# When the second layer of an expert runs, and when the weights' product is spread between the experts

## The chip, the cores and the metric

The kernel runs on one core of one Trainium2 chip. The metric is the device time of one execution in microseconds (us). Three runs of the kernel before gave 395.93, 396.1 and 394.4, a median of 395.93. Five engines work side by side: TensorE (PE, with its weight loads as PEld), VectorE (DVE), ScalarE (ACT), GpSimd (POOL), and SyncE (SP), which here only issues transfers. Sixteen DMA engines move the data.

## The reference, cut to what matters

Three blocks follow each other on 4608 tokens (8 batches of 576) with 512 features, all in fp32:

```python
# 1. retention: 8 batches, 8 heads, 576 positions, 64 features a head
ret = (q @ k.T / 8) * Dmat          # Dmat[i, j] = gamma_h ** (i - j), 0 above the diagonal
x = ret @ v                         # as 4608 x 512
# 2. soft mixture: 8 experts with 4 slots each
logits = x @ phi                                    # 4608 x 32
d = softmax(logits, over tokens); c = softmax(logits, over slots)
slot_in = d.T @ x                                   # 32 x 512
h = relu(slot_in[e] @ w1[e]); slot_out[e] = h @ w2[e]   # w1[e] 512 x 1024, w2[e] 1024 x 512
x = c @ slot_out                                    # 4608 x 512
# 3. bilinear block
out = (((x @ m1) * (x @ m2)) @ w3) @ w_out          # m1, m2 512 x 1024, w3 1024 x 1024, w_out 1024 x 512
```

The inputs of m1, m2, w3 and w_out come as 64-bit floats, the expert weights as fp32.

## The kernel before, in words

The kernel has four stages. Stage 1 (`for u in range(NU)`) does the retention, 36 units of 128 tokens, with the softmax over tokens beside it. Stage 2 is the loop over the eight experts (`for e in range(NE)`, L938 to L965), about 171 to 250 us in the profile; the change is in it alone. Stage 3 (about 250 to 285 us) makes use of the rank: after the experts, x is c times a 32-row matrix, so the bilinear block needs only products of pairs of slot rows. They are formed on VectorE (`pairs`, L1040 to L1047) and multiplied with the product of the last two weights, `w3 @ w_out` (`g_mm`, L1055). Stage 4 (285 to 395 us) does nine blocks of 512 tokens with the result (L1121 to L1136).

In stage 2 three kinds of work share TensorE, in the order in which the loop writes them; every engine and SP's list of transfers work in program order, nothing is sorted afterwards.

* **The experts.** `emit_l1(e)` (L602) multiplies the 4 slots with the first layer's weights, 16 matmuls, which the trace shows as 32; ScalarE applies relu (L607), VectorE transposes (L615, called at step t = 1). `emit_l2(e)` (L622) is the second layer, 8 matmuls shown as 16. An expert's weights are eight transfers of 512 KB (L583, `load_expert`), four for each layer. They go into a ring of buffers that were q, k, v and other tiles in stage 1 (hence names as `q<-in_ew`, `xts<-in_ew`). A buffer goes back to the list `free` when the layer that reads it is written down, so the transfer into it waits for that layer's matmuls; the first buffer of each second layer leaves the ring for good (`wplaces`).
* **The weights' product.** `emit_Ws(n)` writes n of 64 groups of `w3 @ w_out`, three matmuls of 128 x 512 each (L564): weights are held as a high and a low half, and three of the four cross products are taken. Eight groups fill a PSUM bank, which ScalarE and VectorE then evict (L572, L573). Three groups stand ahead of the experts.
* **The conversion.** A piece of w3 (64-bit, 512 KB, L479) is turned into fp32 and its two halves by two operations on ScalarE (L502, L504), three on VectorE (L503, L505, L497), an addition on GpSimd (L523), a copy on ScalarE (L528) and a subtraction on GpSimd (L533). `convert(n)` writes n of the five first ones; `tick()` writes the addition, the copy and the subtraction at a later step. The transfer of the next piece is written directly behind the last VectorE operation of an earlier one (L497), since it overwrites the raw data.

Each expert has four steps t = 0 to 3. At each step the loop runs `tick`, issues what transfers it can, calls `emit_Ws` up to a target number of groups, then the second layer at its step, then one step of the token softmax (`soft`: PE transposes L409 and L390, VectorE L396 and L397, ScalarE L398 and L410), then `convert`. SP's list is in that order too: a transfer whose wait isn't over keeps all later ones back. Its transfers use eight semaphores in turn, so that a transfer also waits for the eighth before it to have landed.

Of the kernel before, what the change touches and what calls it, by code (L numbers as in the profile page):

```python
# [31 lines left out]
def retention_softmoe_bilinear(  # L32
# [65 lines left out]
    def place(tag, name=None, dt=F32):  # L98
        t = new("place", name or tag, 1024, dt, tag=tag)
        all_places.append((t, tag))  # L100
        return t

    def tag_of(t):
        return next(g for x, g in all_places if x is t)
# [310 lines left out]
    def store_expt(last):  # L415
        for T, n in ((0, 8), (8, 1)):
            for g in range(4):
                for o in (0, 32):
                    i = nc.sync.dma_start(
                        out=bass.AP(expt.tensor, expt.offset + 512 * (64 * T + o) + 128 * g, [[512, 32], [64 * 512, n], [1, 128]]),  # L420
                        in_=L["et"][T // 8][32 * g:32 * g + 32, 0:n],
                    )
                    if T + g + o == 0:
                        after(i, last)
# [56 lines left out]
    def load_pieces():  # L481
        while nl[0] < len(pieces) and nl[0] < done[0] + NRAW:
            load_piece(nl[0])
            nl[0] += 1
# [4 lines left out]
    def conv_list(i):  # L489
        t, p = value(turn[i]), parts[i % 2]  # L490
        w = raws[i % NRAW].rearrange("p (n w) -> p n w", w=2)
        lo, hi = w.bitcast(U32)[:, :, 0], w.bitcast(U32)[:, :, 1]
        tu = t.bitcast(U32)
        v = nc.vector

        def last():
            v.scalar_tensor_tensor(out=tu, in0=hi, scalar=0xC0000000, in1=tu, op0=ALU.bitwise_and, op1=ALU.bitwise_or)  # L497
            done[0] += 1
            adds.append(lambda: add(i))

        return [
            lambda: nc.scalar.activation(out=t, in_=w[:, :, 1], func=ACTF.Abs),  # L502
            lambda: v.tensor_scalar(out=t, in0=t, scalar1=W_MIN, scalar2=W_MAX, op0=ALU.max, op1=ALU.min),  # L503
            lambda: nc.scalar.activation(out=p.bitcast(I32), in_=lo, func=ACTF.Copy, scale=2.0 ** -29),  # L504
            lambda: v.tensor_scalar(out=tu, in0=tu, scalar1=3, scalar2=0x3FFFFFFF, op0=ALU.logical_shift_left, op1=ALU.bitwise_and),  # L505
            last,
        ]

    def run_conv(n):
        for _ in range(min(n, len(conv_ops))):  # L510
            conv_ops.pop(0)()
# [32 lines left out]
    nsplit, nW = [0], [0]  # L544
# [7 lines left out]
    def emit_Ws(n, lag=1):  # L552
        for _ in range(n):
            i, k = divmod(nW[0], 4)
            if i == 16 or nsplit[0] < min(9 + i + lag, 24):
                return
            nW[0] += 1
            ps = bank[(5, 2)[i // 2 % 2]]
            b = block(w3p, i % 3)
            ah, al = (b[:, o + 128 * k:o + 128 * k + 128] for o in (0, 512))  # L560
            k8 = 4 * (i % 2) + k
            bh, bl = (t[:, 512 * k8:512 * k8 + 512] for t in (woh, wol))
            for part, (x, y) in enumerate(((ah, bh), (ah, bl), (al, bh))):
                nc.tensor.matmul(out=ps, lhsT=x, rhs=y, start=(k8 == 0 and part == 0), stop=(k8 == 7 and part == 2))  # L564
            if k8 == 7:
                evicts.append(lambda cb=i // 2, ps=ps: evict(cb, ps))

    def evict(cb, ps):
        t = place(tag_of(wplaces[cb]), f"w{cb}", F32R)
        wh.append(t[:, 0:512])  # L570
        wl.append(t[:, 512:1024])
        nc.scalar.copy(out=wh[cb], in_=ps)  # L572
        nc.vector.tensor_tensor(out=wl[cb], in0=ps, in1=wh[cb], op=ALU.subtract)  # L573
# [4 lines left out]
    def load_expert(n=1):  # L578
        loads = []
        while n and free and len(ew) < 8 * NE:  # L580
            e, j = divmod(len(ew), 8)
            ew.append(free.pop(0))
            loads.append(nc.sync.dma_start(out=ew[-1], in_=(ew1, ew2)[j // 4][e][:, 1024 * (j % 4):1024 * (j % 4) + 1024]))  # L583
            n -= 1
        return loads
# [12 lines left out]
    def emit_l1(e):  # L598
        ps = bank[e % 2]
        for k in range(4):  # L600
            for g in range(4):
                last = nc.tensor.matmul(  # L602
                    out=ps[32 * g:32 * g + 32, 0:256], lhsT=slotm[:, 128 * e + 32 * k:128 * e + 32 * k + 32],
                    rhs=ew[8 * e + k][:, 256 * g:256 * g + 256], start=(k == 0), stop=(k == 3), skip_group_check=True,
                )
        hr = tmp.tile([128, 256], F32, tag="h0", name="hr")
        nc.scalar.activation(out=hr, in_=ps[:, 0:256], func=ACTF.Relu)  # L607
        hr_of[e] = hr
        free.extend(ew[8 * e:8 * e + 4])
        return last  # L610

    def emit_turned(e):
        hr = hr_of[e]
        ht = tmp.tile([128, 256], F32, tag="h1", name="ht")
        nc.vector.transpose(out=ht, in_=hr)  # L615
        ht_of[e] = ht

    def emit_l2(e):
        ht = ht_of[e]
        for cb in range(8):  # L620
            qd = cb % 4
            nc.tensor.matmul(  # L622
                out=bank[4][32 * qd:32 * qd + 32], lhsT=ht[:, 32 * cb:32 * cb + 32], rhs=ew[8 * e + 4 + cb // 2][:, 512 * (cb % 2):512 * (cb % 2) + 512],
                start=(e == 0 and cb < 4), stop=(e == 7 and cb >= 4), skip_group_check=True,
            )
        free.extend(ew[8 * e + 4:8 * e + 8])
# [28 lines left out]
    with tc.manual_schedule():  # L655
# [75 lines left out]
        def can_conv():  # L731
            if nconv[0] == nl[0]:
                return False
            j = turn[nconv[0]]
            return 8 <= j < N3 or nth(j) < nsplit[0] + 3
# [167 lines left out]
        def convert(n):  # L903
            while n:
                if not conv_ops:
                    if not can_conv():
                        return
                    conv_ops.extend(conv_list(nconv[0]))
                    nconv[0] += 1
                    run_conv(1)  # L910
                run_conv(1)
                n -= 1
                if adds:
                    load_pieces()

        def tick():
            run(subs)
            run_copies()
            run(adds)
            run(evicts)  # L920
# [4 lines left out]
        def soft():  # L925
            T, step = divmod(nsoft[0], 2)
            if T < NT:
                nsoft[0] += 1
                if step == 0:
                    emit_csoft(T)  # L930
                else:
                    emit_expt(T)
                    if T + 1 < NT:
                        emit_turn(T + 1)
# [3 lines left out]
        for e in range(NE):  # L938
            load_expert(8)
            last = emit_l1(e)  # L940
            if e == NE - 1:
                store_expt(last)
            if e == 0:

                free[:] = [t for t in free if not any(t is x for x in ring)]
                second = tag_of(free.pop(0))
                etp = [place("ew0", "et0"), place(second, "et1")]
                L["et"] = [t.rearrange("p (t n) -> p t n", n=128) for t in etp]
                L["soft"] = [etp[1][:, o:o + 128].rearrange("p (g s) -> p g s", g=4) for o in (512, 640)]
            for t in range(4):  # L950
                tick()
                if t == 1:
                    emit_turned(e)
                load_expert(8)
                emit_Ws(max(0, min(55, 4 + (4 * e + t + 1) * 52 // 28) - nW[0]))
                if e == NE - 1 and t == 1:
                    emit_Ws(3, 0)
                if t == 2:
                    emit_l2(e)
                    if len(wplaces) < 8:  # L960
                        wplaces.append(free.pop(0))
                    load_expert(8)
                while e < NE - 1 and nsoft[0] <= (4 * e + t) * 18 // 28:
                    soft()
                convert(2 + t % 2)  # L965
        emit_Ws(1, 0)
        so = acc
        nc.scalar.copy(out=so[:, 0:256], in_=bank[4][:, 0:256])
# [245 lines left out]
```

## Time and profile before

| what | value |
|---|---|
| runs (us) | 395.93, 396.1, 394.4, median 395.93 |
| the profiled execution, its own time | 397.17 us, span 395.4 us |
| PE busy | 377.4 us (95%), 4447 matmuls |
| PEld busy | 284.3 us (72%) |
| DVE, ACT, POOL busy | 254.5, 198.8, 172.5 us (64, 50, 44%) |
| chain that ended last | PE 72%, DMA 13%, DVE 11% |
| main DMA queue | 107.85 MB, 85.3% of 16 engines |
| granted clock of TensorE | 0.999 |

The page gives busy shares over the whole span; the four stages have different limits. The chain that ended last is followed back from the last instruction, so it names what released each step. The profiled execution lies 1.24 us above the median of the runs.

### The profile page before, as it was taken

The page shows a single profiled execution, that of the slowest core. Times are in us where ns is not written, and L with a number is a line of the kernel's source. Part 1 is how long each engine was busy: PE and PEld are TensorE (multiplying, and loading weights), DVE is VectorE, ACT ScalarE, POOL GpSimd, SP SyncE. Part 2 cuts the span into 40 slices and gives each one's busy share as a digit, 9 for nine tenths or more (in the row PEclk, how much of TensorE's full clock was granted, in tenths as well). Part 3 has the DMA queues.
Part 4 walks back from the last instruction along what each step waited for, and adds up shares of the span by engine and source line. Part 5 has one row for each costly group of instructions (what it writes and reads, how often), then busy time and mean ns, then how long its engine had stood idle before and what let it go on. Part 6 is the DMA issues. An engine that isn't in the chain of part 4 may idle for free.

```text
span 395.4 us, 10962 instructions
## 1 busy us (share of the span) xinstructions
PE 377.4 (95%) x4447; PEld 284.3 (72%) x4447; DVE 254.5 (64%) x432; ACT 198.8 (50%) x424; POOL 172.5 (44%) x158
## 2 busy tenths in 40 slices
PE   6999998999998999899999998999999999999995
PEld 3889786878887886566555553578687777788774
DVE  3458999899887988545776552299766443555410
ACT  2347695788676785414544521235444353444332
POOL 2732765675554554113554431037634434553420
PEclk9999999999999999999999999999999999999999
DMA  7999999799889999997999999692269979999543
GB/s 236 333 330 322 308 352 321 246 385 389 277 278 324 337 319 346 336 409 264 390 400 409 410 408 381 140 219 51 61 127 209 230 190 246 236 218 211 155 98 98
DMA packets 48211, 108.75 MB, mean 275 GB/s; under 512 B 7584, under 2 KB 10016, under 8 KB 48160
## 3 DMA queue, kind: packets, MB, share of 16 engines
q1 hardware_dynamic: 47008, 107.85, 85.3%
q8 instruction: 35, 0.57, 0.6%
q10 hardware_dynamic: 1152, 0.20, 0.3%
q14 instruction: 16, 0.13, 0.1%
HBM read 97.41 MB, written 10.62 MB: 273 GB/s over the span
## 4 chain that ended last, share of the span: by engine, by line
PE 72%; DMA 13%; DVE 11%; ACT 1%; issue 1%; SPq 0%; ACTq 0%; DVEq 0%
PE bank L1130 9%; PE bank L1132 8%; PE bank L1131 8%; PE scores L253 7%; PE output L282 7%; PE bank L564 7%; DMA v<-in_ew 5%; PE output L316 4%; PE state L296 3%; DMA q<-in_ew 3%; DMA st<-in_ew 3%; PE bank L622 2%; PE bank L602 2%; PE pair L215 2%; DMA v<-in_v 2%; PE bank L1121 2%
## 5 line engine op out<-in xcount | busy, mean ns | idle before, releaser
L646 POOL TENSOR_TENSOR cc<-mw_sb,cc 128x512 fp32r<-128x512 f32 x36 | 46.0, 1298 | 56.9 <-ACT cc L645 55.6
L564 PE MATMUL bank<-wop,w3p 128*128 128x512 f32 x192 | 50.9, 407 | 0.0
L523 POOL TENSOR_TENSOR vals<-vals,msb 128x512 int32<-128x512 int32 x24 | 30.8, 1285 | 42.7 <-DVE vals L497 36.8
L263 DVE TENSOR_TENSOR pm<-scores,msb 128x1024 f32<-128x1024 f32 x31 | 37.8, 1220 | 14.6 <-PE scores L253 14.3
L564 PEld LDWEIGHTS bank<-wop,w3p 128*128 128x128 f32 x192 | 34.1, 188 | 15.0 <-issue 8.7
L645 ACT CAST cc<-mw_sb 128x512 fp32r<-128x512 f32 x36 | 22.2, 616 | 43.6 <-DVE mw_sb L644 34.8
L1130 PE MATMUL bank<-w3p,cc 128*128 128x512 f32 x108 | 43.1, 399 | 0.0
L1132 PE MATMUL bank<-w3p,cc 128*128 128x512 f32 x108 | 42.1, 390 | 0.0
L1131 PE MATMUL bank<-w3p,cc 128*128 128x512 f32 x108 | 42.1, 390 | 0.0
L253 PE MATMUL scores<-q,kt 64*128 64x128 f32 x496 | 37.3, 290 | 1.2 <-issue 1.2
L644 DVE TENSOR_TENSOR mw_sb<-lga,raw 128x512 f32<-128x512 f32 x32 | 29.3, 954 | 12.3 <-POOL cc L646 12.1
L282 PE MATMUL output<-pm,v 128*64 128x128 f32 x512 | 35.6, 279 | 1.7 <-issue 1.7
L533 POOL TENSOR_TENSOR w3p<-vals,w3p 128x512 fp32r<-128x512 f32 x16 | 21.1, 1317 | 35.0 <-ACT w3p L528 32.3
L523 POOL TENSOR_TENSOR mw_sb<-mw_sb,msb 128x512 int32<-128x512 int32 x16 | 20.4, 1275 | 31.6 <-DVE mw_sb L497 18.5
L253 PEld LDWEIGHTS scores<-q,kt 64*128 64x128 f32 x496 | 31.1, 192 | 4.2 <-issue 2.4
L1134 ACT ACTIVATE mw_sb<-bank,rz 128x512 f32<-128x512 f32 x36 | 24.7, 685 | 18.7 <-PE bank L1132 9.6
L282 PEld LDWEIGHTS output<-pm,v 128*64 128x64 f32 x512 | 27.5, 136 | 7.0 <-issue 5.8
L220 ACT COPY kt<-pair 128x512 f32<-128x512 f32 x26 | 15.2, 586 | 27.6 <-PE pair L219 27.6
L504 ACT ACTIVATE msb<-raw 128x512 int32<-128x512 uint32 x40 | 27.9, 697 | 0.0
L192 POOL TENSOR_TENSOR k<-kr,msb 128x512 f32<-128x512 f32 (+1 forms) x30 | 25.8, 883 | 3.9 <-PE one L205 2.8
L1130 PEld LDWEIGHTS bank<-w3p,cc 128*128 128x128 f32 x108 | 20.3, 188 | 7.1 <-issue 2.9
L1132 PEld LDWEIGHTS bank<-w3p,cc 128*128 128x128 f32 x108 | 20.3, 188 | 4.4
(226 smaller groups left out, 770.9 us busy)
## 6 DMA issues: line engine op xcount, KB each, us to landing
q<-in_q SPq DMA_DIRECT2D x20, 512.0 KB, 6.4
raw<-expt SPq DMA_DIRECT2D x36, 256.0 KB, 4.3
kr<-in_v SPq DMA_DIRECT2D x16, 512.0 KB, 6.1
v<-in_v SPq DMA_DIRECT2D x16, 512.0 KB, 6.5
raw<-in_m SPq DMA_DIRECT2D x16, 512.0 KB, 6.0
raw<-in_w SPq DMA_DIRECT2D x16, 512.0 KB, 6.7
out_x<-mw_sb SPq DMA_DIRECT2D x64, 128.0 KB, 2.4
q<-in_ew SPq DMA_DIRECT2D x14, 512.0 KB, 10.1
```

The lines of the kernel that those rows point to most:

```text
L192: (nc.vector if first else nc.gpsimd).tensor_tensor(out=Ks[:, :, 0:m, h], in0=K[:, 1 - h, :, 0:m], in1=ktab(c, h)[:, 0:m].unsqueeze(1).uns ...
L253: last = nc.tensor.matmul(out=ps[:, p], lhsT=ktb[u % 2][a, p], rhs=Q[a, :, x, p], start=True, stop=True)
L263: nc.vector.tensor_tensor(out=p_places[u % 2].rearrange("p (g t) -> p g t", g=8), in0=(pair if u == 1 else scores).rearrange("p (g t) -> p ...
L282: last = nc.tensor.matmul(out=xt_view(p)[side(p, h)], lhsT=v_tile(u)[:, 1 - h, x, p], rhs=p_main(u)[:, h, p], start=(block_of(u) == 0 and ...
L504: lambda: nc.scalar.activation(out=p.bitcast(I32), in_=lo, func=ACTF.Copy, scale=2.0 ** -29),
L523: nc.gpsimd.tensor_tensor(out=ti, in0=ti, in1=parts[i % 2].bitcast(I32), op=ALU.add)
L564: nc.tensor.matmul(out=ps, lhsT=x, rhs=y, start=(k8 == 0 and part == 0), stop=(k8 == 7 and part == 2))
L644: eng.tensor_tensor(out=e, in0=x, in1=y[:, m], op=ALU.mult)
L646: nc.gpsimd.tensor_tensor(out=cl[m], in0=e, in1=ch[m], op=ALU.subtract)
L1130: nc.tensor.matmul(out=ob, lhsT=ch[m][:, sl], rhs=gh[m], start=False, stop=False)
L1131: nc.tensor.matmul(out=ob, lhsT=ch[m][:, sl], rhs=gl[m], start=False, stop=False)
L1132: nc.tensor.matmul(out=ob, lhsT=cl[m][:, sl], rhs=gh[m], start=False, stop=(m == 3))
```

## The change

Two numbers of the schedule in stage 2 and the step of one call change, and with them the conversion's pace. The target of groups of the product after step `4 * e + t + 1` was a straight line, `4 + step * 52 // 28`; it is now a line with three pieces: 4, 5, 5, 5 in expert 0, then 6, 7, 7, 7 in expert 1, then 48 groups over the 20 steps of experts 2 to 6. The second layer moves from step t = 2 to t = 3, behind all groups of its expert and directly ahead of the next expert's first layer (the step of the token softmax stands between in some). `convert` writes three operations a step in place of two and three in turn.

```diff
-                emit_Ws(max(0, min(55, 4 + (4 * e + t + 1) * 52 // 28) - nW[0]))
+                step = 4 * e + t + 1
+                emit_Ws(max(0, (min(5, 3 + step), min(7, 1 + step), min(55, 7 + (step - 8) * 48 // 20))[min(e, 2)] - nW[0]))
                 if e == NE - 1 and t == 1:
                     emit_Ws(3, 0)
-                if t == 2:
+                if t == 3:
                     emit_l2(e)
                     if len(wplaces) < 8:
                         wplaces.append(free.pop(0))
                     load_expert(8)
                 while e < NE - 1 and nsoft[0] <= (4 * e + t) * 18 // 28:
                     soft()
-                convert(2 + t % 2)
+                convert(3)
```

TensorE's order at the first two experts, before (`bank0` and `bank1` receive first layers, `bank4` second layers, `bank5` and `bank2` the product):

```order
L602 MATMUL bank0_2623<-kr1_105,slotm_83 32x256 x4
L564 MATMUL bank5_2628<-wop_78,w3p_79 128x512 x15
L564 MATMUL bank2_2625<-wop_78,w3p_79 128x512 x3
L622 MATMUL bank4_2627<-k2_108,ht_2766 32x512 x2
L622 MATMUL bank4_2627<-q2_100,ht_2766 32x512 x2
L622 MATMUL bank4_2627<-kt_97,ht_2766 32x512 x2
L622 MATMUL bank4_2627<-v2_103,ht_2766 32x512 x2
L409 MATMUL bank7_2630<-cst_72,et1_2752 128x128
L390 MATMUL bank3_2626<-cst_72,lga_73 128x128
L564 MATMUL bank2_2625<-wop_78,w3p_79 128x512 x6
L602 MATMUL bank1_2624<-k0_106,slotm_83 32x256 x4
```

And the same place now:

```order
L602 MATMUL bank0_2623<-kr1_105,slotm_83 32x256 x4
L564 MATMUL bank5_2628<-wop_78,w3p_79 128x512 x6
L409 MATMUL bank7_2630<-cst_72,et1_2752 128x128
L390 MATMUL bank3_2626<-cst_72,lga_73 128x128
L622 MATMUL bank4_2627<-k2_108,ht_2763 32x512 x2
L622 MATMUL bank4_2627<-q2_100,ht_2763 32x512 x2
L622 MATMUL bank4_2627<-kt_97,ht_2763 32x512 x2
L622 MATMUL bank4_2627<-v2_103,ht_2763 32x512 x2
L602 MATMUL bank1_2624<-k0_106,slotm_83 32x256 x4
```

Between the first layers of experts 0 and 1 stood 24 matmuls of the product, now 6; for experts 1 to 2 it was 21 and is 6. The 33 missing ones come back in experts 2 to 6: between first layers stand 27, 30, 27, 30, 30 where 24, 21, 24, 21, 21 stood (156 in all both times, and 9 more in expert 7).

SP's list from the last weights of expert 2 on, before (`in_ew1` and `in_ew2` are the two layers' weights, `in_w3` a piece for the conversion):

```order
L583 DMA v2_103<-in_ew2 128x1024
L479 DMA raw_80<-in_w3 128x512
L583 DMA k0_106<-in_ew1 128x1024
L583 DMA q0_98<-in_ew1 128x1024
L583 DMA v0_101<-in_ew1 128x1024
L583 DMA q1_99<-in_ew1 128x1024
L479 DMA raw_80<-in_w3 128x512
L583 DMA pm0_94<-in_ew2 128x1024
L583 DMA pm1_95<-in_ew2 128x1024
L583 DMA st_96<-in_ew2 128x1024
L479 DMA raw_80<-in_w3 128x512
L583 DMA xts0_89<-in_ew2 128x1024
```

And now:

```order
L583 DMA v2_103<-in_ew2 128x1024
L479 DMA raw_80<-in_w3 128x512
L583 DMA k0_106<-in_ew1 128x1024
L583 DMA q0_98<-in_ew1 128x1024
L583 DMA v0_101<-in_ew1 128x1024
L583 DMA q1_99<-in_ew1 128x1024
L583 DMA pm0_94<-in_ew2 128x1024
L583 DMA pm1_95<-in_ew2 128x1024
L583 DMA st_96<-in_ew2 128x1024
L583 DMA xts0_89<-in_ew2 128x1024
L583 DMA xts1_90<-in_ew1 128x1024
L583 DMA xts2_91<-in_ew1 128x1024
```

The six pieces of w3 are the same; the first keeps its place, the other five moved behind later weights. The weights keep their own order and their buffers.

ScalarE's rows around the first layer of expert 6, before and now (`hr` is that layer's relu, `raw` a piece of w3 as it came):

```order
L502 ACTIVATE vals_82<-raw_80 128x512
L504 ACTIVATE msb_84<-raw_80 128x512
L528 CAST w3p_79<-vals_82 128x512
L398 ACTIVATE et1_2752<-et1_2752 128x128
L607 ACTIVATE hr_3292<-bank0_2623 128x256
```

```order
L398 ACTIVATE et1_2752<-et1_2752 128x128
L502 ACTIVATE vals_82<-raw_80 128x512
L504 ACTIVATE msb_84<-raw_80 128x512
L502 ACTIVATE vals_82<-raw_80 128x512
L504 ACTIVATE msb_84<-raw_80 128x512
L607 ACTIVATE hr_3277<-bank0_2623 128x256
```

The relu stands behind one piece's two ScalarE operations before, and behind two pieces' now; they are the last two of the 16 pieces.

## Rows read from the trace of the kernel before

**Rows 1.** Busy time by stretch, one row for an expert, clock, DMA share, GB/s.

```profile
171.30:181.10 9.80, 9.80 (x75) 5.85 (x74) 3.19 (x8) 2.59 (x7) 1.28 (x1) 1.00 0.86 331
181.10:190.30 9.20, 9.20 (x72) 5.32 (x71) 6.11 (x14) 5.79 (x13) 5.04 (x4) 1.00 0.88 319
...
209.60:219.40 9.80, 9.80 (x75) 5.85 (x74) 5.97 (x15) 4.11 (x10) 4.91 (x4) 1.00 1.03 408
219.40:230.00 10.60, 9.62 (x75) 5.22 (x74) 6.47 (x14) 4.42 (x10) 4.09 (x4) 1.00 1.03 409
230.00:240.30 10.30, 9.66 (x73) 5.34 (x72) 4.36 (x13) 2.60 (x7) 3.85 (x3) 1.00 1.03 408
```

**Rows 2.** Timeline of PE: start, us, engine, line, operation, [idle before <-releaser].

```profile
173.14 4.42 PE L564 MATMUL bank<-wop,w3p 128*128 128x512 f32 x18
177.49 0.62 PE L622 MATMUL bank<-k,ht 128*32 128x512 f32 x2
...
219.41 0.64 PE L602 MATMUL bank<-v,slotm 128*32 128x256 f32 x8
...
222.66 2.34 PE L564 MATMUL bank<-wop,w3p 128*128 128x512 f32 x9
...
229.99 0.64 PE L602 MATMUL bank<-q,slotm 128*32 128x256 f32 x8
...
232.90 1.69 PE L564 MATMUL bank<-wop,w3p 128*128 128x512 f32 x6
...
240.34 1.08 PE L602 MATMUL bank<-xts,slotm 128*32 128x256 f32 x16
...
243.90 2.37 PE L564 MATMUL bank<-wop,w3p 128*128 128x512 f32 x9
246.20 0.62 PE L622 MATMUL bank<-v,ht 128*32 128x512 f32 x2
...
249.43 0.98 PE L564 MATMUL bank<-wop,w3p 128*128 128x512 f32 x3
```

**Rows 3.** The chain that ended last, in order of time: start, us, what.

```profile
171.35 1.86 PE bank L602 x32
...
177.56 1.85 PE bank L622 x16
...
238.56 9.84 DMA v<-in_ew
248.45 1.05 PE bank L622 x4
```

**Rows 4.** Timeline of SP: start and us of each issue.

```profile
173.28 0.37 SPq L583 DMA_DIRECT2D kr<-in_ew  x1
178.62 0.33 SPq L583 DMA_DIRECT2D q<-in_ew  x1
...
184.11 0.33 SPq L479 DMA_DIRECT2D raw<-in_w  x1
...
199.12 0.33 SPq L583 DMA_DIRECT2D q<-in_ew  x1
200.40 0.33 SPq L583 DMA_DIRECT2D kt<-in_ew  x1
```

**Rows 5.** Line L583 from 160 to 250 us, from issue to landing.

```profile
DMA to landing us min/median/max: 4.0/10.2/11.0
```

**Rows 6.** Timelines of ACT and DVE, expert 1's conversion and transpose.

```profile
179.71 0.27 ACT L410 COPY et<-bank 128x128 f32<-128x128 f32 x1 [5.17 <-PE bank L409]
179.87 0.66 ACT L502 ACTIVATE vals<-raw 128x512 f32<-128x512 f32 x1
...
183.35 0.69 DVE L497 SCALAR_TENSOR_TENSOR vals<-raw,vals 128x512 uint32<-128x512 uint32 x1
...
185.85 0.44 DVE L615 STREAM_TRANSPOSE ht<-hr 128x256 f32<-128x256 f32 x1
```

**Rows 7.** Waits of SP's queue: for whom, us in total, times, longest.

```profile
SPq L479 <- DVE vals L497: 13.7, 6, 3.5
```

## The prediction

> **What bounds the kernel now.** I read the busy time by stretch first, then TensorE's timeline, then the chain of waits and SP's own queue. In the stage of the experts TensorE is never idle for the first five experts: 9.80 us busy of 9.80, 9.20 of 9.20, until 219.4 us [rows 1]. From there it waits for weights. Undisturbed, a first layer takes 1.86 us and a second one 1.85 us [rows 3]. The first layers of experts 5, 6 and 7 last 222.66 - 219.41 = 3.25, 232.90 - 229.99 = 2.91 and 243.90 - 240.34 = 3.56 us, and expert 7's second layer 249.43 - 246.20 = 3.23 us [rows 2]. The excess is 1.39 + 1.05 + 1.70 + 1.38 = 5.5 us. What they wait for is the transfers: the chain runs through the last weights, issued at 238.56 and landing 9.84 us later, and 1.05 us of matmuls behind them [rows 3].
>
> The transfers run at full rate there: 408 or 409 GB/s with all DMA engines busy [rows 1], one issue each 200.40 - 199.12 = 1.28 us [rows 4], and 10.2 us from issue to landing since eight are in the queue [rows 5]. They are late because of what was lost earlier. In the first two experts they moved only 331 and 319 GB/s [rows 1]. SP's timeline says why: nothing is issued between 173.28 and 178.62, and little until 184.11 [rows 4], since the buffers are still held by layers that TensorE has not come to, behind up to 18 matmuls of the product [rows 2]. So TensorE is the bound for five experts, the transfers for three, and the second debt is made in the first two experts.
>
> **The change part by part.**
>
> *Work.* Nothing is added or removed: 165 matmuls of the product, 64 transfers of weights, 16 conversions, as before. All of the effect is order. When the first layer of expert 0 ends, all weights of the first two experts and three transfers of the third have been issued; by SP's list 45 transfers of weights and 6 pieces of w3 are still to come.
>
> *Experts 0 and 1 lose 11 groups.* Eighteen product matmuls take 177.49 - 173.14 = 4.35 us, 0.242 each [rows 2]. With 6 in place of 18 between the layers, expert 0's second layer starts at 171.3 + 1.86 + 6 x 0.242 + 0.2 (softmax pair) = 174.8, not 177.5; expert 1's first layer ends at 178.5, not 183.0; its second layer runs 180.2 to 182.1, not 187.6 to 189.4; expert 2's first layer ends at 184, not 192.2. Each of these ends frees buffers, so the transfers into them are issued 2.7, 4.5, 7.3 and 8 us earlier. The queue then never runs dry behind expert 0. What is to be won is what the stretches lack: (9.8 x (408 - 331) + 9.2 x (408 - 319)) / 408 = 1.85 + 2.0 = 3.9 us [rows 1]. The low end, if the hole that begins before the first early release stays, is the second stretch alone, 2.0 us. A transfer needs at least 4.0 us from issue to landing [rows 5], so one issued at about 175.9 comes a little late for a queue that got its last entry at 173.28; I leave about 0.6 us of the first stretch and take 3.3.
>
> *What the gain can be at most.* TensorE's waits are 5.5 us; 3.3 leaves about 2.2 us of waits with it in the last experts, so the transfers stay the bound and TensorE keeps that much in reserve for waits that the change adds.
>
> *Second layer behind all groups.* It frees its buffers later within its expert. The one that matters is expert 6, whose second layer frees the last transfer's buffer. TensorE comes to it, without waits, at 171.3 + 7 x 1.86 + 6 x 1.85 + 156 x 0.242 + about 1.8 (softmax pairs and switches) = 235.0, and with those 2.2 us of waits at 237.2; the first buffer is free 1.05 us later, at 238.3, against 238.56. The landing is due at 248.4 - 3.3 = 245.1, and 6.8 us are more than the least of 4.0. Cost nothing, with 2.8 us of cover; beyond it each us costs one.
>
> *Less cover for the relu and the transpose.* In expert 1 the transpose came at 185.85 [rows 6], 2.8 us behind the first layer's end at 183.0; now only 6 matmuls and the softmax pair, 1.7 us, stand before the second layer. TensorE may wait up to 1.6 us there. It costs nothing at the end: that second layer's buffers, free at 182 to 184, are wanted for transfers that land after 190, and the 2.2 us of reserve take the wait. Behind the transpose on VectorE stand only small operations of the softmax. Bounds 0 and 1.6 us within the reserve; I take 0.
>
> *Conversion and pieces.* From expert 2 on 30 matmuls fall between first layers, 2.5 pieces per expert, and 12 operations per expert write 2.4. VectorE was busy 6.5 us of some 10 at most in these stretches, ScalarE 5.8 and GpSimd 5.0 [rows 1], so the same work in fewer experts fits. Counted back from a last landing at 245.1 at 1.28 us a transfer, with 15 transfers behind the last piece, the five moved pieces land at about 207, 213, 214, 225 and 226 us; by the same forward count of TensorE the product needs the first of them near 223 and the last two after 240. Cost nothing.
>
> *Everything behind the last weights* (stages 3 and 4) keeps its order and moves along.
>
> Sum: 397.17 - 3.3 = 393.9 us for the profiled execution. That one was 1.24 us above the median of the runs, so against 395.93 it is 392.6 us.
>
> **The rivals.**
>
> *The queue stands still as before (no change).* In SP's list the first piece keeps its place ahead of expert 3's weights, and its transfer waits for L497; SP waited 13.7 us in all for that operation [rows 7]. If L497 still comes at 183.35 [rows 6], the weights behind the piece are issued after 184.1 as before, the second stretch stays poor, and at most the first's 1.3 us are won: 394.6. For it speaks the longest such wait, 3.5 us. Against it: L497 is the end of a chain that starts when L410 has its transposition from TensorE, L502 starting 0.16 us behind it [rows 6], and that transposition now stands ahead of the second layer, at 174.8 in place of 179.3. The chain took 184.04 - 179.87 = 4.2 us, so it ends by 179.4.
>
> *More is won.* If the holes cost more than the stretches show, and TensorE's reserve is used as well, the limit is its 5.5 us: 390.4. Full rate would have to be above the 409 GB/s of the rows; a middle value of 4.6 us gives 391.3.
>
> *A piece blocks the weights (slower).* Five pieces now stand between later weights, two pairs directly behind one another. Each waits for a L497 of a conversion that itself waits for a block of the product to be used. SP's list is in order, so all weights behind wait too. The queue holds eight transfers, 10.2 us, and a new one needs 4.0 us, so a blockade is free up to 6.2 us and costs its length beyond that. Were the 13.7 us of such waits to come in one place, 7.5 us would be lost, 4.2 more than is won; half way, 2.5 us slower: 398.4. It decides from a blockade of 9.5 us on. The same lateness would hold expert 6's relu, which now stands behind two pieces on ScalarE. Against it: the fifth and sixth L497 are due near 210 and their transfers have their turn near 214.
>
> *The rate is not there.* The 408 GB/s are held for 30 us in a row [rows 1]. The Trainium skill, in "DMA: Bandwidth & Descriptors", Measured, says that transfers from HBM are bound at about 358 GB/s for a core; by that the two stretches lacked only (9.8 x 27 + 9.2 x 39) / 358 = 1.7 us, and the kernel would end at 394.2. By that rule the change is hardly worth measuring; the trace doesn't agree, since three stretches stand 50 GB/s above it, and the measurement decides.
>
> **How the numbers follow.** About 0.5%, or 2.0 us, is what a measurement of this kernel can tell from no change. My forecast 392.6 has a chance of 0.64, with its own range from 392.0 (all 3.9 us) to 393.9 (2.0 us). The queue standing still, 394.6: 0.20. More, 391.3: 0.08. A blockade, 398.4: 0.05. The rate, 394.2: 0.03. Faster is the forecast without its weakest tenth, and "more": 0.58 + 0.08, and a little for runs that scatter by themselves, 0.69. Slower is 0.06 with that scatter, the same 0.25. The range that leaves no more than 2 in 10 out goes from 391.0 to 395.1, as the runs before lie 1.7 us apart.
>
> **What would show it.** Right: the first two experts' stretches move about 400 GB/s; the first piece is issued near 179; the last weights land near 245; TensorE's excess in the layers of experts 5 to 7 falls from 5.5 to about 2.2 us; and stages 3 and 4 last as long as before. Wrong: if a gap in SP's issues longer than 6 us remains, if the product's matmuls wait for their halves in experts 3 to 6, or if the transfers end 3 us earlier and stage 3 gives it back.

## The result and the profile after

The changed kernel takes 392.77 us (median of 16 runs, 390.94 to 395.1) beside 395.76 us before (16 runs, 394.0 to 398.17): ratio 0.9917, 95% interval 0.9894 to 0.9939, which is some 3.3 us; the medians lie 3.0 us apart. The forecast was 392.6 us, 3.3 below the 395.93 that it started from. Here and below the medians are of all runs, while ratios and intervals leave out slow ones, those more than 1.5% above the fastest of their kernel. The profiled execution is 391.39 us long, 5.78 us less than that of before. Stages in the two, by the first matmul of L602, the matmul behind the last L622 and the first matmul of the final stage:

| stretch (us) | before | after |
|---|---|---|
| up to expert 0's first layer (not changed) | 171.28 | 169.62 |
| the eight experts | 78.15 | 74.05 |
| up to the final stage's first matmul | 35.36 | 35.35 |
| from there to the span's end | 110.6 | 110.7 |

Of the 5.78 us, 1.66 fell ahead of anything that was changed: these two executions happened to differ there. The change is in the experts, 4.10 us, and nothing is given back behind them.

Busy time by stretch, experts 0, 1, 5, 6 and 7 (answers to [rows 1]; columns as there):

```profile
169.60:175.05 5.45, 5.45 (x58) 2.81 (x61) 2.76 (x8) 2.19 (x6) 1.28 (x1) 1.00 1.03 417
175.05:180.40 5.35, 5.35 (x60) 2.78 (x56) 4.22 (x15) 1.70 (x5) 1.29 (x1) 1.00 1.02 391
...
212.17:224.20 12.03, 11.28 (x84) 6.98 (x80) 7.83 (x19) 6.69 (x14) 7.34 (x6) 1.00 1.02 409
224.20:237.40 13.20, 11.93 (x89) 6.93 (x84) 5.72 (x16) 3.81 (x9) 6.40 (x5) 1.00 1.03 409
237.40:243.70 6.30, 6.30 (x59) 3.07 (x58) 1.14 (x2) 1.24 (x3) 0.00 (x0) 1.00 0.99 316
```

The light experts are little more than half as long and the transfers no longer fall to 331 and 319 GB/s. TensorE is idle in experts 5 and 6, with transfers at 409 GB/s: the transfers still bound the end.

TensorE's timeline (answers to [rows 2]):

```profile
171.48 1.68 PE L564 MATMUL bank<-wop,w3p 128*128 128x512 f32 x6
...
212.17 0.61 PE L602 MATMUL bank<-v,slotm 128*32 128x256 f32 x8
...
214.61 0.64 PE L602 MATMUL bank<-st,slotm 128*32 128x256 f32 x8 [0.64 <-DMA st<-in_ew]
215.18 3.72 PE L564 MATMUL bank<-wop,w3p 128*128 128x512 f32 x15
...
224.21 0.61 PE L602 MATMUL bank<-q,slotm 128*32 128x256 f32 x8
...
227.38 0.64 PE L602 MATMUL bank<-q,slotm 128*32 128x256 f32 x8 [0.63 <-DMA q<-in_ew]
227.95 1.66 PE L564 MATMUL bank<-wop,w3p 128*128 128x512 f32 x6
...
241.49 0.62 PE L622 MATMUL bank<-v,ht 128*32 128x512 f32 x2
...
242.69 0.62 PE L622 MATMUL bank<-v,ht 128*32 128x512 f32 x2
...
243.67 0.96 PE L564 MATMUL bank<-wop,w3p 128*128 128x512 f32 x3
```

The first layers of experts 5 and 6 last 215.18 - 212.17 = 3.01 and 227.95 - 224.21 = 3.74 us, 1.15 and 1.88 us over 1.86; expert 7's first layer has no excess, its second layer 243.67 - 241.49 = 2.18 us, 0.33 over. Together 3.36 us, where it was 5.5.

The chain that ended last (answers to [rows 3]):

```profile
173.38 1.85 PE bank L622 x16
175.23 1.73 PE bank L602 x32
...
217.19 10.15 DMA q<-in_ew
227.38 0.64 PE bank L602 x8
```

It still runs through a weight's transfer, now expert 6's. In this view a first layer directly behind a second one takes 1.73 us in place of 1.86, so the two together 3.58 in place of 3.71.

SP's timeline (answers to [rows 4]):

```profile
171.61 0.37 SPq L583 DMA_DIRECT2D kr<-in_ew  x1
174.43 0.33 SPq L583 DMA_DIRECT2D q<-in_ew  x1
...
176.72 0.33 SPq L479 DMA_DIRECT2D raw<-in_w  x1
177.14 0.77 SPq L583 DMA_DIRECT2D k<-in_ew  x1
...
236.34 0.33 SPq L583 DMA_DIRECT2D v<-in_ew  x1
```

And SP's wait for L497 between 140 and 260 us (answer to [rows 7]):

```profile
SPq L479 <- DVE vals L497: 5.1, 4, 2.4
```

The gap of 5.34 us behind 173.28 is now 2.82 us, and the first piece of w3 goes out 7.1 us behind expert 0's first matmul, not 12.8 (184.11 - 171.28).

### The profile page after: what moved, and what is told of

It reads as the page before. It is cut to its first block, busy times and chain, and to the rows that moved or that the text cites. A ratio compares the mean times of both kernels' runs of the same rounds, so it can differ in the third digit from the quotient of the medians.

```text
span 389.7 us, 10959 instructions
## 1 busy us (share of the span) xinstructions
PE 373.0 (96%) x4447; PEld 284.2 (73%) x4447; DVE 253.3 (65%) x432; ACT 199.3 (51%) x424; POOL 172.4 (44%) x158
## 4 chain that ended last, share of the span: by engine, by line
PE 68%; DMA 15%; DVE 13%; issue 1%; ACT 1%; POOL 1%; SPq 0%; ACTq 0%; POOLq 0%; DVEq 0%
PE bank L1131 9%; PE bank L1133 8%; PE bank L1132 8%; PE scores L253 6%; PE output L282 6%; DMA xts<-in_ew 5%; PE bank L564 5%; DMA q<-in_ew 5%; PE output L316 4%; DMA kr<-in_v 4%; PE state L296 3%; PE bank L602 2%; PE bank L622 2%; PE one L356 2%; PE pair L215 2%; PE bank L1122 2%
## 5 line engine op out<-in xcount | busy, mean ns | idle before, releaser
L564 PE MATMUL bank<-wop,w3p 128*128 128x512 f32 x192 | 49.0, 402 | 0.0
L564 PEld LDWEIGHTS bank<-wop,w3p 128*128 128x128 f32 x192 | 34.6, 188 | 11.9 <-issue 5.4
L253 PE MATMUL scores<-q,kt 64*128 64x128 f32 x496 | 36.4, 285 | 0.7 <-issue 0.7
L253 PEld LDWEIGHTS scores<-q,kt 64*128 64x128 f32 x496 | 30.3, 187 | 3.5 <-issue 1.7
```

Source lines behind the costliest of these rows:

```text
L253: last = nc.tensor.matmul(out=ps[:, p], lhsT=ktb[u % 2][a, p], rhs=Q[a, :, x, p], start=True, stop=True)
```

## The experiments

Two theories stood against each other. *Queue theory*, the prediction's: the transfers are late at the end because their queue ran dry early, and the light first experts stop that. *TensorE theory*: the 165 matmuls are the same, but they come in fewer blocks (14 in place of 20, counted to the end of the stage) and five first layers stand directly behind second ones, so TensorE itself needs less time.

### The three parts, each alone

```diff
 # e1_product_only: the kernel before, and only
-emit_Ws(max(0, min(55, 4 + (4 * e + t + 1) * 52 // 28) - nW[0]))
+step = 4 * e + t + 1
+emit_Ws(max(0, (min(5, 3 + step), min(7, 1 + step), min(55, 7 + (step - 8) * 48 // 20))[min(e, 2)] - nW[0]))
 # e2_layer_only: the kernel before, and only
-if t == 2:
+if t == 3:
 # e3_convert_only: the kernel before, and only
-convert(2 + t % 2)
+convert(3)
```

> Only the targets of the product change; the second layer stays at t = 2, the conversion at two and three operations. Queue theory (what is won is won by the transfers, because the first two experts give up 11 groups and their buffers come free earlier): nearly the whole gain, ratio 0.991 to 0.993, stage of the experts from 78.15 to 74 to 74.6 us, last weights landing within 0.5 us of where they land in the changed kernel. TensorE theory (what is won is matmul time: the changed kernel has 14 blocks of the product in place of 20 and five first layers directly behind second layers, some 0.2 us and 0.13 us each): 17 blocks and one such first layer, 0.8 us, ratio 0.998.

> Only the second layer moves to t = 3; the product keeps its straight line. Queue theory: the heavy first two experts hold their buffers as long as before, ratio 0.999 to 1.001, stage 77.7 to 78.5 us, the hole in SP's issues behind 173 us (of before) still there; TensorE's time falls, but its waits in experts 5 to 7 grow by as much. TensorE theory: 16 blocks in place of 20 and five first layers directly behind second ones, 4 x 0.2 + 5 x 0.13 = 1.5 us, ratio 0.996.

> Only the conversion's pace changes, to three operations a step. Queue theory: the pieces' transfers may come a little earlier, the buffers of the weights do not; ratio 0.999 to 1.001, stage 78 us. TensorE theory: 20 blocks as before, also 1.000. A third theory, that the gain is made by the pieces' new places among the transfers: ratio 0.995 or less.

Measured: the targets alone 392.44 us, ratio 0.990 (0.986 to 0.994), stage 74.20 us. The layer alone 397.52 us, 1.0025 (0.9995 to 1.0055); its profiled execution lost 5 us ahead of the experts and had a granted clock of 0.5 for some 3 us within them, so its stage of 77.36 us says little. Nor does a lower clock hide a gain in its runs: the four whose mean granted clock was 0.996 or more average 396.9 us, the twenty such runs of before 396.5 us. The conversion alone 396.19 us, 1.0007 (0.998 to 1.004), stage 76.89 us. The targets are the whole gain, as the queue theory has it; with them alone the last weights land 73.2 us behind the stage's start, in the changed kernel 73.0 us, and 77.1 us before.

The run with the conversion alone does not test the pieces' new places among the transfers, as its expectation meant it to: its trace shows the six pieces at the places of before. It is the targets that move them, since the conversion of a piece waits for groups of the product: with the targets alone five pieces go out behind later weights, as in the changed kernel. That the new places alone win nothing is therefore not shown by a run of its own. What the traces do show is that SP's waits for L497, through which a piece holds the weights behind it, do not go with the gain: 13.7 us before, 7.0 with the targets alone, 9.1 with the layer alone, and of the two runs below 10.6 us in the one that wins and 7.4 in the one that doesn't.

In the stage of the targets alone TensorE has only some 1.9 us of waits left (layers of 2.25, 1.99 and 3.26 us where 1.86 is undisturbed), 1.4 less than the changed kernel, and the same length: matmul time saved came out as waiting.

### Which of the two experts

```diff
 # the changed kernel, with another expression for the target (the rest of the line is cut)
 # e4_first_light
+(min(5, 3 + step) if e == 0 else min(55, 5 + (step - 4) * 50 // 24))
 # e5_second_light
+(4 + step * 52 // 28, min(13, 7 + step), min(55, 13 + (step - 8) * 42 // 20))[min(e, 2)]
```

> The changed kernel, but only expert 0 is light (6 matmuls of the product behind its first layer); expert 1 has 24 and the rest follow in a straight line to the same 55 groups. Sum by stretches (the two stretches' deficits are separate, as the prediction added them): 1.3 to 1.85 us are won, ratio 0.995 to 0.997, stage 76 us. Bridge theory (there is one hole, which begins when the eight transfers of the queue have landed; expert 0's buffers, free 2.7 us earlier, and expert 1's first layer's, free 4.5 us earlier, put twelve transfers in, 12 x 1.28 = 15.4 us, which bridge a heavy expert 1): nearly all is won, ratio 0.991 to 0.993, stage 74 to 74.6 us, no issue gap of SP over 6 us between 174 and 195 us.

> The counterpart: expert 0 keeps its heavy load (24 matmuls ahead of its second layer), expert 1 is light (6), the rest in a straight line to 55 groups. Sum by stretches: the second stretch's 2.0 us are won, less up to 0.5 us since expert 0's second layer comes 1.5 us later, ratio 0.995 to 0.996, stage 76 us. Bridge theory: the queue has run dry before expert 0's second layer frees anything, and a light expert 1 comes too late for it, ratio 0.998 to 1.001, stage 77 to 78 us.

Measured: expert 0 alone light 392.82 us, 0.9904 (0.987 to 0.994), stage 73.63 us: the whole gain. Expert 1 alone light 396.1 us, 0.9989 (0.9963 to 1.0014), stage 77.42 us: nothing. The first 20 us of the experts tell them apart (busy time of each engine, last column GB/s). The kernel before:

```profile
171.28:191.28 20.00, 20.00 (x166) 11.80 (x169) 10.21 (x25) 8.39 (x18) 7.30 (x6) 1.00 0.88 327
```

The changed kernel:

```profile
169.62:189.62 20.00, 20.00 (x182) 11.95 (x185) 10.14 (x32) 7.49 (x18) 4.13 (x4) 1.00 1.02 397
```

Expert 0 alone light:

```profile
172.40:192.40 20.00, 20.00 (x178) 12.47 (x178) 9.77 (x29) 8.04 (x19) 5.95 (x5) 1.00 1.01 394
```

Expert 1 alone light:

```profile
170.19:190.19 20.00, 19.27 (x175) 11.78 (x175) 12.63 (x28) 8.19 (x20) 7.34 (x6) 1.00 0.85 317
```

Against 408 GB/s they lack 20 x 81 / 408 = 4.0, 0.5, 0.7 and 4.5 us; the differences to before are 3.4, 3.3 and -0.5 us, where the runs' ratios say 3.3, 3.8 and 0.4. SP's timeline says why. With expert 0 light:

```profile
174.40 0.37 SPq L583 DMA_DIRECT2D kr<-in_ew  x1
177.20 0.33 SPq L583 DMA_DIRECT2D q<-in_ew  x1
...
182.58 0.38 SPq L583 DMA_DIRECT2D q<-in_ew  x1
186.69 1.15 SPq L583 DMA_DIRECT2D pm<-in_ew  x2
```

With expert 1 light:

```profile
172.19 0.37 SPq L583 DMA_DIRECT2D kr<-in_ew  x1
179.11 0.33 SPq L583 DMA_DIRECT2D q<-in_ew  x1
...
183.45 0.40 SPq L583 DMA_DIRECT2D q<-in_ew  x1
186.41 0.33 SPq L479 DMA_DIRECT2D raw<-in_w  x1
```

A gap of 4.1 us (182.58 to 186.69) costs next to nothing once the queue is filled: the transfers issued on either side of it landed at 191.02, 192.23, 193.51 and 194.79 us, some 1.28 us apart, which is the full rate; one of 6.9 us (172.19 to 179.11) comes when little is in it. What frees buffers in time are expert 0's second layer and expert 1's first one, and the product that stands ahead of both is expert 0's. Expert 1's delays only its own second layer and what follows. With expert 1 alone light, expert 0's second layer also stands behind 24 matmuls in place of 18, which this run can't separate.

### The transfers taken away

```diff
 # h1_before_half (of before), h2_after_half (of the changed kernel)
+h = 1024 if len(ew) < 20 else 512
-loads.append(nc.sync.dma_start(out=ew[-1], in_=(ew1, ew2)[j // 4][e][:, 1024 * (j % 4):1024 * (j % 4) + 1024]))
+loads.append(nc.sync.dma_start(out=ew[-1][:, 0:h], in_=(ew1, ew2)[j // 4][e][:, 1024 * (j % 4):1024 * (j % 4) + h]))
```

> The kernel before, where the experts' weights from the 20th transfer on load only the first half of their columns (the rest of the buffer keeps what it held): 44 transfers move half the data, all instructions stay. This takes the transfers away as a bound, so that TensorE's order alone shows. Queue theory: TensorE's 5.5 us of waits in experts 5 to 7 go, stage 72.65 us, ratio 0.986. If the waits were not for the transfers' rate, the stage stays near 78 us.

> The changed kernel with the same half transfers. TensorE theory in pure form (all that was won is matmul time): 4 us below the other half-transfer kernel. Queue theory: with the transfers out of the way the change is worth only what the order saves on TensorE, 6 blocks of the product and five first layers directly behind second ones, 78.15 - 5.5 = 72.65 against 74.05 - 3.36 = 70.69 us, so 1.9 us; ratio to the kernel before 0.981. If the blocks cost nothing, as the prediction had it: no difference.

These two kernels leave out half of the data of 45 transfers (64 - 19; the expectation counts 44). Measured: 391.42 us, 0.988 (0.983 to 0.993), and 389.7 us, 0.983 (0.978 to 0.988). Busy time of the whole stage of the experts, in the order before:

```profile
170.54:243.11 72.57, 72.57 (x567) 42.33 (x567) 42.39 (x99) 29.83 (x66) 30.11 (x23) 1.00 0.72 238
```

And in the new order:

```profile
170.28:240.94 70.66, 70.66 (x567) 43.49 (x567) 42.71 (x99) 30.19 (x66) 30.39 (x23) 1.00 0.73 248
```

TensorE is busy without a break in both. 72.57 is the 78.15 of before less the 5.5 us of waits (72.65), so the waits were all for the transfers' rate. And with no transfer in the way the same 567 matmuls still take 1.91 us less in the new order. That saving is real, but in the full kernel the transfers take it back as waits.

### TensorE's waits put to use

```diff
 # v2_all_groups (and v2_again), of the changed kernel
-min(55, 7 + (step - 8) * 48 // 20)
+min(59, 7 + (step - 8) * 52 // 20)     (in expert 6 with the lag 0)
-emit_Ws(4, 0)
 # v3_first_light_all, as v2 with
+(min(5, 3 + step) if e == 0 else min(59, 5 + (step - 4) * 54 // 24))
 # v4_filled, as v2, and where emit_Ws(4, 0) stood
+for _ in range(6):
+    nc.tensor.matmul(out=bank[5], lhsT=block(w3p, 0)[:, 384:512], rhs=woh[:, 3584:4096], start=True, stop=True)
```

> The changed kernel with four more groups (12 matmuls, 12 x 0.2275 = 2.7 us) in experts 2 to 6, taken from behind the experts: their last four stood behind the 64 matmuls of L997 and their copy and subtraction (L572, L573) in VectorE's chain of stage 3. Queue theory: the transfers bound the last experts and TensorE has 3.4 us of waits there, so the added work costs nothing to 0.4 us, stage of the experts 74.05 to 74.5 us; stage 3 loses the subtraction's 0.69 us and up to 0.5 us of waiting, 34.3 to 34.8 in place of 35.42; in all 0.5 to 1 us faster than the changed kernel, ratio to the kernel before 0.989 to 0.991. TensorE theory: the stage grows by the whole 2.7 us, and the kernel is 1.5 to 2 us slower than the changed one, ratio 0.996 to 0.998.

> The changed kernel once more, on one chip with the two others of this set. Ratio to the kernel before 0.990 to 0.993; stage of the experts 73.6 to 74.5 us, stage 3 35.4 us.

> The version with four more groups in experts 2 to 6, again. Queue theory: TensorE's waits still hold the 2.7 us, so stage of the experts 73.9 to 74.5 us, stage 3 34.6 us; 0.3 to 0.8 us faster than the changed kernel, ratio 0.988 to 0.991. If its first profile was a lucky one, the same time as the changed kernel, 0.991 to 0.993.

> Both findings together: only expert 0 light, then a straight line to 59 groups, and none left behind L997. The transfers' hole is bridged as with expert 0 light alone, stage 73.5 to 74.3 us (TensorE's own work is 70.7 + 2.7 = 73.4 us at least), stage 3 34.6 us; 0.4 to 1.2 us faster than the changed kernel, ratio 0.987 to 0.991.

> The version with four more groups in experts 2 to 6, and six matmuls whose result nothing reads in the gap of 1.67 us that it left on TensorE behind L997. Clock theory (in the repeated profile TensorE stood still there, then its granted clock was 0.50 for some 3 us and stage 3 lasted 36.15 in place of 34.60 us): with the gap filled the clock stays at 1.00, stage 3 34.6 us, stage of the experts 73.9 to 74.2 us, median 0.7 us below the changed kernel's, ratio 0.988 to 0.990. Rival (the fall of the clock is an accident of single executions, or the filled matmuls delay what follows): stage 3 still 36 us, or 35 us and more with the clock at 1.00.

The lag is the number of further pieces that must be split before a group is written; without it expert 6 can take the groups of the newest piece. Measured, with the profiled execution's two stages:

| kernel | median us | ratio to before | experts | up to the final stage |
|---|---|---|---|---|
| changed, again | 392.44 | 0.9894 (0.985 to 0.994) | 74.57 | 35.35 |
| four groups earlier | 392.48 | 0.9894 (0.986 to 0.993) | 74.16 | 34.60 |
| four groups earlier, again | 392.78 | 0.9887 (0.984 to 0.994) | 73.86 | 36.15 |
| four groups earlier, expert 0 alone light | 393.95 | 0.9898 (0.984 to 0.996) | 74.21 | 36.13 |
| four groups earlier, the gap filled | 393.32 | 0.9851 (0.979 to 0.992) | 74.09 | 34.60 |

The experts' stage takes 12 matmuls more, 2.7 us of work, at no cost: TensorE's waits there were idle time, which the TensorE theory excludes. The next stage then is 0.75 us shorter in the first execution, as expected, and 0.8 us longer in two others, where 34.6 us had been expected. TensorE's timeline behind L997 in such a one, the second run of that kernel:

```profile
253.79 1.46 PE L1055 MATMUL bank<-w,wop 128*128 128x512 f32 x4 [1.67 <-ACT wop L1043]
255.75 3.45 PE L1055 MATMUL bank<-w,wop 128*128 128x512 f32 x8 [0.50 <-ACT wop L1043]
```

Its busy time there, with the granted clock in the last column but two:

```profile
256.00:259.20 3.20, 3.20 (x9) 2.37 (x9) 3.17 (x8) 0.60 (x2) 0.93 (x1) 0.52 1.04 211
```

The first execution has the same two gaps (1.67 and 0.49 us), but its eight matmuls take 2.11 us in place of 3.45, and the same stretch reads:

```profile
256.00:259.20 3.20, 3.16 (x14) 2.28 (x15) 3.14 (x7) 0.88 (x2) 0.94 (x1) 1.00 1.06 220
```

So the four groups that were moved away had also kept TensorE busy. Without them it stood still, and in two of the three profiled executions without them the granted clock then fell to 0.5, that is to 1.2 GHz, for some 3 us. With the gap filled by six matmuls the one execution profiled kept 1.00 there:

```profile
256.00:259.20 3.20, 2.96 (x13) 2.19 (x14) 2.95 (x7) 0.87 (x3) 0.94 (x1) 1.00 1.07 222
```

One is too few to say that the filling prevents it, all the more as the clock fell in other profiled executions far from these groups: at 89.4 us in the filled version itself, at 127.1 us in e4_first_light, each time for some 3 us and behind an idle gap of TensorE of 2.06 and 1.69 us. That the opened gaps caused the two falls is likely and not shown. The medians of these versions can't be told from the changed kernel's: none is shown to beat it, though each had been expected to by 0.3 to 1.2 us.

## Why the prediction came out right, step by step

- *What bounds the kernel* held. TensorE has no gap in the first five experts, the transfers bound the last, and the waits there were for their rate: halved transfers take them all away.
- *The 3.9 us that the first two experts lose* held as a sum: 4.0 us by the first 20 us of before, 0.5 left after, 3.4 won, where 3.3 was forecast and the ratio says 3.3. The profiled stage shows 4.10 us; the excess of 0.7 us is within what single executions differ by (the changed kernel's second profile, 74.57 us, shows 3.58; the conversion alone changed nothing in the runs, and its profiled stage was 1.26 us shorter).
- *Its division between the two experts* failed. The prediction added the stretches' deficits, 1.85 and 2.0 us, as if each were that of its own product. By that sum expert 0 alone light would have won 1.3 to 1.85 us and expert 1 alone light up to 2.0, as their expectations work out; they won 3.8 us and 0.4 (interval -0.6 to 1.5) by the ratios. The second stretch's loss also comes from expert 0's product, which delays expert 1's first layer. Eleven groups were taken out; the five of expert 1 need not have moved. The change made both experts light, so the wrong division didn't show in the total: in this the prediction was lucky. Its low end of 2.0 us, the second stretch alone, rests on the same division.
- *A queue that got its last entry at 173.28*, and the 0.6 us left for it: the first early issue came 2.82 us behind the last, and the stretch moved 391 GB/s. What is left, 0.5 us, has the size forecast.
- *"Nothing is added or removed", so no effect on TensorE's work*, is the term that was mis-sized: 1.91 us by the halved transfers. It did not reach the end because the transfers bound there; so the waits left are 3.36 us, not 2.2, and the total was right without it, because the prediction had the transfers as the bound and they were. Had TensorE been the bound, the forecast would have been 1.9 us too high.
- *Second layer behind all groups*: no cost. The last transfer was issued at 236.34, 5.1 us behind the one before it, and landed at 242.65, 1.28 us behind the landing of that one: just when its turn at full rate came, so the late issue cost nothing, as forecast. The last pairs of L622 at 242.69 still waited for it. Alone the move wins nothing.
- *Relu, transpose, conversion*: no cost. No matmul of the product waits for a piece. (`convert` writes a new piece's first operation without counting it, so 12 counted operations are up to three pieces an expert, not 2.4.) In the changed kernel TensorE doesn't wait for expert 1's transpose, and in the run with expert 1 alone light 0.73 us, within the 1.6 us bound.
- *The rivals.* The queue didn't stand still: its waits for L497 fell from 13.7 to 5.1 us, and the first piece left 7.1 us behind the stage's start. No piece blocked the weights: the longest such wait is 2.4 us. (The prediction's price for half such a blockade, 2.5 us, does not follow from its 4.2: half of that is 2.1.) *More* was not shown either: 4.1 us in the profiled stage, 3.3 by the runs. The rate is there, 409 GB/s in the 40 us behind the first 20:

```profile
189.62:229.62 40.00, 37.98 (x292) 23.11 (x284) 27.80 (x59) 19.47 (x40) 21.18 (x17) 1.00 1.03 409
```

  The Trainium skill, in "DMA: Bandwidth & Descriptors", Where 436 GB/s comes from, has transfers from HBM bound at about 358 GB/s for a core. That does not hold for this kernel on one core. The Trainium skill's section Measured, which the prediction names for it, gives 358 GB/s for two cores of a pair that both stream, and lists 425 GB/s for a 16 MB transfer on a core alone, which the trace is nearer to.

## What to carry to other kernels

When transfers bound the end of a stage, look for the place where their queue first ran dry, here five experts earlier, and for the work that stands ahead of the layer whose buffers it needs: one layer freed early there can be the whole gain. Before counting a saving on an engine, see whether it is the bound: here 1.9 us of matmul time went into waits, and 2.7 us of matmuls could be added to them for nothing. Work that only fills a gap may also hold TensorE's clock, which two of three traces here suggest; look at the granted clock behind a gap that a move opens.

## What was not expected of the hardware

- The same 567 matmuls cost TensorE 72.57 us in the old order and 70.66 us in the new one, both with halved transfers. Five first layers directly behind second ones, at 1.73 in place of 1.86 us, are 0.65 of the 1.91 us; by estimate the rest is about 0.2 us for each of the six blocks of the product fewer. No run changes the number of blocks alone.
- Gaps of 1.67 and 0.50 us, with 1.46 us of matmuls between them, were followed in two of three executions by a granted clock of 0.5 (1.2 GHz) for some 3 us, and the stage was then 36.15 - 34.60 = 1.55 us longer; in the third, with the same gaps, it stayed. The Trainium skill, in "TensorE: Matmul & The Clock Gate", A second HAM failure mode: psum-queue depth-cycling, tells of a kernel whose short idles between groups of matmuls let the clock swing; the two traces agree as far as one fall each goes, the third doesn't.
- In one trace a transfer queue that had run dry did not come back to its full rate at once. With expert 1 alone light, the stretches from 5 to 10, 10 to 15 and 15 to 20 us behind the experts' start read (last two columns DMA share and GB/s):

```profile
175.19:180.19 5.00, 5.00 (x42) 2.84 (x44) 2.04 (x4) 2.39 (x5) 1.29 (x1) 1.00 0.43 164
180.19:185.19 5.00, 4.27 (x48) 2.36 (x44) 3.01 (x8) 2.37 (x6) 2.44 (x2) 1.00 0.94 321
185.19:190.19 5.00, 5.00 (x56) 3.03 (x45) 4.83 (x11) 2.23 (x6) 2.33 (x3) 1.00 1.01 369
```

  Between 180.35 and 183.45 SP issued six transfers, and still the second of these stretches moved 321 GB/s and the third 369, not 409, with the DMA engines busy 94% and 101% of the time. Part of the 321 is the 3.9 us that the first transfer took to land; why the third stretch is short as well stays open.
